# All casts of two weight matrices on GpSimd, no small copies on it in the first block, and a new order of the first block's steps

## The chip, the cores and the metric

The kernel runs on one core of a Trainium2 chip. Its engines are PE (TensorE: matrix products, with its weight loads as PEld), DVE (VectorE), ACT (ScalarE), POOL (GpSimd) and SP (SyncE, which here only issues loads). They run side by side, each takes its own instructions strictly in order, and they wait for each other by semaphores. The metric is the device time in microseconds, as the median of several runs, before and after the change. Matmul results land in PSUM; every other on-chip tensor lies in SBUF.

## What is computed

Retention (a decaying linear attention) over 4 batches, 8 heads, 768 positions in blocks of 64, and then a channel mix on its output `x`:

```python
x_prev = np.concatenate([np.zeros((B, 1, D)), x[:, :-1, :]], axis=1)
xk = mu_k * x + (1.0 - mu_k) * x_prev
xr = mu_r * x + (1.0 - mu_r) * x_prev
k = np.maximum(xk @ w_k, 0.0)              # 512 -> 1024
v = k * k @ w_v                            # 1024 -> 512
r = 1.0 / (1.0 + np.exp(-(xr @ w_r)))      # 512 -> 512
return r * v
```

## The kernel before

**Tiling.** The 768 positions go through in six blocks `n` of 128, each block for the four pairs of heads `hp`. The large products (`k_product`, `r_part`, `v_part`, lines 434, 423, 460) split each fp32 operand in a high and a low part and take three matmuls (high x high, high x low, low x high), so a matmul on `xl` needs the low part of the activation.

**The order.** Nothing is scheduled: the string `ORDER` (line 508) lists steps, a letter with two indices each, and the loop at line 494 issues them one after the other. All instructions of one engine stay in that order (the recording helper is line 33, so every row of the profile has that line). The letters used below, with the functions and what they put on which engine:

- `L`, `N`, `M`: loads of a pair's queries and keys, values, and keys by rows. SP issues all loads in one queue (`load_hp`, `load_qv`, `load_first`).
- `T0`, `T2` (`powers`, line 184): decay tables `Dt` and `LP`. PE transposes, DVE and ACT copy out.
- `A` scores on PE, `a` decay: in block 0 two DVE multiplications `mv<-sc,Dt` of a PSUM tile with `Dt`. `q` decays queries: DVE `mv<-qv,LP`, of two SBUF operands.
- `B` values on PE, `b` a copy of the result to SBUF (`raw<-xp`, ACT, block 0 alone), `k` ACT decays keys, `U` sums on PE, `u` state on ACT.
- `e`, `E` (`mix_prev`, line 392): ACT scales the attention output into `ts`, shifted by one column, for the k and the r branch; then POOL copies column 0 of `ts` from `lastw` (the last column of the block before) and saves the new last column in `lastw`. `f`, `F` (`mix`): DVE finishes `ts`. `y`, `x` (`split_x`): ACT writes the high part `xh`, DVE the low part `xl`; tiles 0 to 3 are the k branch's (`y`), 4 to 7 the r branch's (`x`).
- `S`, `c`, `C`, `D`: a weight is loaded as raw 16-bit words of its fp32 values (`S`), the upper halves are cast to fp16 into one of two tiles `top` (`conv_top`, line 245: `top<-raw`), DVE combines them by shift and OR (`conv_bits`: `raw<-raw,top`), and `split` makes high (ACT) and low part (DVE, `wk<-raw,wk` or `wr<-raw,wr`). Pieces k4 to k7 and r0 to r3 have 512 elements a partition, k2, k3 and v0 to v3 have 1024. Here POOL casts k4 to k7 and ACT casts the others.
- `G`, `K`: products with w_k, in block 0 pair by pair (`G`), `R`, `Q`: products with w_r, `V`: products with w_v.

There are two tiles `top`, taken in turn, so a cast waits for the OR of the cast two before it.

Of the kernel before, what the change touches and what calls it, by code (L numbers as in the profile page):

```python
# [7 lines left out]
F32 = mybir.dt.float32  # L8
# [7 lines left out]
ALU = mybir.AluOpType  # L16

B, H, S, D = 4, 8, 768, 64
HP = H // 2
NT = S // 128  # L20
# [16 lines left out]
def tile_retention_moe(  # L37
# [26 lines left out]
    tensor, vector, scalar, gpsimd, sync = (  # L64
        InOrder(tc, e) for e in (tc.nc.tensor, tc.nc.vector, tc.nc.scalar, tc.nc.gpsimd, tc.nc.sync))
# [6 lines left out]
    tiny = ctx.enter_context(tc.tile_pool(name="tiny", bufs=1))  # L72
# [22 lines left out]
    Dt = const.tile([128, H, 128], F32, name="Dt")  # L95
    LP = const.tile([128, HP, 64], F32, name="LP")
    LC = tiny.tile([128, HP], F32, name="LC")
    lastw = tiny.tile([128, 2, HP, B], F32, name="lastw")
    omu = tiny.tile([128, 2, HP], F32, name="omu")

    first = {}
# [72 lines left out]
    vector.tensor_tensor(rows.rearrange("p (c a) -> p c a", a=8), now[:, 8:25].rearrange("p (c o) -> p c o", o=1).broadcast_to([128, 17, 8]),  # L174
                         lows.rearrange("p (o a) -> p o a", o=1).broadcast_to([128, 17, 8]), op=ALU.mult)
    vector.tensor_scalar(omu, mus, -1.0, 1.0, op0=ALU.mult, op1=ALU.add)
    gpsimd.memset(lastw, 0.0)
    gpsimd.tensor_copy(lone[:, 512:640].rearrange("p (a x) -> p a x", a=2),
                       parity.rearrange("p (a o) -> p a o", o=1).broadcast_to([128, 2, 64]))

# [42 lines left out]
    def part(kind, i):  # L223
        if kind == "r" or i >= 4:
            j, c = divmod(i % 4, 2)
            c = slice(c, c + 1)
        else:
            j, c = i, slice(0, 2)
        key = f"{kind}{j}"
        if key not in raw:  # L230
            raw[key] = home(RAW[key], "raw", True)
        return key, c, raw[key].rearrange("p (c x) -> p c x", c=2)[:, c]
# [8 lines left out]
    def tops_of(kind, i, t):  # L241
        top = tops[turn.setdefault((kind, i), len(turn) % 2)]
        return top[:, 0:t.shape[1] * 512].rearrange("p (c o) h -> p c o h", o=512)

    def conv_top(kind, i):
        t = part(kind, i)[2]
        copy = gpsimd.tensor_copy if kind == "k" and i >= 4 else scalar.copy
        copy(tops_of(kind, i, t)[:, :, :, 1].bitcast(F16), t[:, :, 2::4].bitcast(BF16))

    def words(t):  # L250
# [13 lines left out]
    scs, mvs, us, xps, ts = {}, {}, {}, {}, {}  # L264
# [127 lines left out]
    def mix_prev(n, which, hp):  # L392
        ts[n, which, hp] = t = tiny.tile([128, B, 129], F32, tag=f"ts{which}", name="ts", bufs=2)
        scalar.activation(t[:, :, 1:129], xps[n, hp], AF.Copy, scale=omu[:, which, hp:hp + 1])
        gpsimd.tensor_copy(t[:, :, 0], lastw[:, which, hp, :])
        if n + 1 < NT:
            gpsimd.tensor_copy(lastw[:, which, hp, :], t[:, :, 128])

    def mix(n, which, hp):
        t = ts[n, which, hp]  # L400
        o = t[:, :, 0:128]
        vector.scalar_tensor_tensor(o, xps[n, hp], mus[:, which, hp:hp + 1], t[:, :, 0:128],
                                    op0=ALU.mult, op1=ALU.add)
# [17 lines left out]
    rps, rt, kps, kfs, k2, vps = {}, {}, {}, {}, {}, {}  # L421
# [60 lines left out]
    def v_out(n, b):  # L482
# [3 lines left out]
    steps = dict(  # L486
        L=load_hp, N=load_qv, A=scores, a=decay, q=decay_queries, k=decay_keys, U=sums, u=even_state, w=odd_state, B=values,
        e=lambda n, hp: mix_prev(n, 0, hp), E=lambda n, hp: mix_prev(n, 1, hp),
        f=lambda n, hp: mix(n, 0, hp), F=lambda n, hp: mix(n, 1, hp),
        y=lambda n, hp: split_x(n, 0, hp), x=lambda n, hp: split_x(n, 1, hp),  # L490
        M=lambda n, hp: load_first(hp, 2), b=keep_raw, G=lambda f, hp: k_product(0, f, hp),
        R=lambda n, hp: r_part(n, hp, 0), Q=lambda n, hp: r_part(n, hp, 1), s=r_out, K=k_part, h=k_square, p=k_split, V=v_part, o=v_out,
        S=stage_part, c=conv_top, C=conv_bits, D=conv_split)
    for step in ORDER.split():
        if step[0] == "T":
# [3 lines left out]
        else:  # L499
            i, j = step[1], int(step[2])  # L500
# [5 lines left out]
CUTS = ((0, 1024, 2048), (0, 1024, 1536, 2048), (0, 1024, 1536, 2048), (0, 1024, 1536, 2048))  # L506

ORDER = """
L00 Z10 L01 M00 M03 T0 k00 Sk4 A00 A01 L02 T2 a00 a01 k03 ck4 M01 B00 A02 Ck4 b00 e00 N01 E00 f00 N02 U00 a02 B01 L03 F00 Dk4
y00 u00 B02 k01 A03 b01 Sk5 x00 N03 M02 G20 G00 b02 ck5 Sk6 Sk7 E01 a03 G30 Ck5 e01 e02 f01 F01 E02 B03 Dk5 y01 f02 G10 ck6 b03  # L510
U01 Ck6 ck7 k02 Ck7 G11 e03 x01 y02 Sk2 G21 Dk6 G31 f03 U02 u01 Sk3 Dk7 U03 G01 ck2 Ck2 E03 G22 y03 Sr1 ck3 G32 Ck3 G02 G12 G33
Sr0 G23 Sr3 Sv3 Dk2 F02 cr1 Dk3 G13 G03 h03 cr0 Sr2 F03 h02 Cr1 Sv0 h00 cr3 Cr0 N11 Sv1 p01 Dr1 cr2 K07 K05 Dr0 h01 Cr3 Cr2 h05
x02 Dr2 Dr3 x03 K04 p00 h04 u03 Q00 N10 h07 Q01 cv0 Sv2 cv3 u02 q11 Q02 Cv0 Q03 L11 Cv3 Dv0 R00 s03 R01 cv1 Cv1 L10 Dv3 R02 k10
R03 K06 k11 s01 A10 A11 q10 Dv1 cv2 Cv2 U10 L12 p02 h06 U11 Dv2 L13 p03 s02 u11 N13 a10 V04 a11 V02 w11 V03 V05 N12 k13 B11 s00
u10 B10 o01 V00 E11 w10 o02 k12 e11 q13 U13 A12 N20 A13 U12 L20 V06 V01 E10 q12 e10 u12 a12 F11 x11 L21 V07 u13 k20 k21 f10 f11
a13 F10 B13 B12 w13 y10 y11 E13 e13 N21 N22 e12 w12 A20 o03 o00 f12 f13 y12 y13 U21 U20 q21 A21 F13 L22 K10 K11 a20 u20 K13 a21
h11 x13 h10 u21 q20 k22 K14 h13 K12 p10 K15 w20 L23 w21 k23 E12 N23 F12 U22 U23 x10 A23 h12 A22 B20 h15 p11 a23 h14 x12 B21 Q10
E21 L30 e20 L31 Q11 Q12 E20 f20 u22 F20 F21 k31 Q13 s12 s13 q23 K17 h17 K16 N31 e21 N30 R10 h16 R11 R12 p12 u23 w22 x21 k30 p13
# [80 lines left out]
```

## Time and profile before

| | |
|---|---|
| median of 3 runs | 397.16 us (396.19 to 399.07) |
| the profiled execution: time, span | 395.83 us, 394.0 us |
| PE busy | 387.8 us (98% of the span), granted clock 1.0 throughout |
| DVE, ACT, POOL busy | 244.3 us (62%), 201.5 us (51%), 34.4 us (9%) |
| the chain that ended last | PE 94%; products with w_v 34%, w_k 32%, w_r 17% |

The span is the time from the first to the last instruction of one execution; 1.8 us lie around it. The chain of waits that ended last is PE itself from 24 us on; only in the first 24 us do other engines and loads stand in it. A row of the timeline gives start and duration in us, engine, line, operation, output<-inputs, shapes, the number of instructions merged in it, and in brackets the engine's idle time before it and what ended that.

### The profile page before, as it was taken

The page shows a single profiled execution, that of the slowest core. Times are in us where ns is not written, and L with a number is a line of the kernel's source. Part 1 is how long each engine was busy: PE and PEld are TensorE (multiplying, and loading weights), DVE is VectorE, ACT ScalarE, POOL GpSimd, SP SyncE. Part 2 cuts the span into 40 slices and gives each one's busy share as a digit, 9 for nine tenths or more (in the row PEclk, how much of TensorE's full clock was granted, in tenths as well). Part 3 has the DMA queues.
Part 4 walks back from the last instruction along what each step waited for, and adds up shares of the span by engine and source line. Part 5 has one row for each costly group of instructions (what it writes and reads, how often), then busy time and mean ns, then how long its engine had stood idle before and what let it go on. Part 6 is the DMA issues. An engine that isn't in the chain of part 4 may idle for free.

```text
span 394.0 us, 8421 instructions
## 1 busy us (share of the span) xinstructions
PE 387.8 (98%) x3532; PEld 321.4 (82%) x3532; DVE 244.3 (62%) x392; ACT 201.5 (51%) x367; POOL 34.4 (9%) x104
## 2 busy tenths in 40 slices
PE   8899999999999999999999999999999999999996
PEld 5777888888888888888888888888888888888886
DVE  6987898699857375876565285855456844222411
ACT  4989997575755362475612347721266542222400
POOL 6540000100110010100100010210000000000000
PEclk9999999999999999999999999999999999999999
DMA  8998934654250081250701070340100001000002
GB/s 302 411 352 300 352 109 137 201 143 166 69 150 0 30 238 57 62 154 0 209 34 57 27 208 8 109 134 27 53 2 2 2 2 55 27 27 2 0 28 80
DMA packets 13606, 42.58 MB, mean 108 GB/s; under 512 B 1920, under 2 KB 2304, under 8 KB 13568
## 3 DMA queue, kind: packets, MB, share of 16 engines
q1 hardware_dynamic: 9824, 35.68, 28.2%
q10 hardware_dynamic: 3744, 6.36, 4.4%
q8 instruction: 28, 0.46, 0.5%
q14 instruction: 10, 0.08, 0.1%
HBM read 35.74 MB, written 6.29 MB: 107 GB/s over the span
## 4 chain that ended last, share of the span: by engine, by line
PE 94%; DVE 1%; POOL 1%; ACT 1%; issue 1%; DMA 0%; POOLq 0%; DVEq 0%
PE vp L33 34%; PE kp L33 32%; PE rp L33 17%; PE xp L33 5%; PE sc L33 3%; PE u L33 3%; POOL lastw L33 1%; PE table L33 0%; DMA smalls<-small 0%; POOL ts L33 0%; ACT ts L33 0%; DVE xl L33 0%; DVE raw L33 0%; POOL pows L33 0%; POOL top L33 0%
## 5 line engine op out<-in xcount | busy, mean ns | idle before, releaser
L33 PE MATMUL vp<-wv,k 128*128 128x512 f32 (+1 forms) x600 | 134.5, 382 | 0.0
L33 PEld LDWEIGHTS vp<-wv,k 128*128 128x128 f32 x600 | 108.9, 188 | 21.9 <-ACT kf L33 0.2
L33 PE MATMUL kp<-xh,wk 128*128 128x512 f32 x384 | 123.3, 391 | 0.0
L33 PEld LDWEIGHTS kp<-xh,wk 128*128 128x128 f32 x384 | 72.1, 188 | 15.7 <-ACT kf L33 0.4
L33 PE MATMUL kp<-xl,wk 128*128 128x512 f32 x192 | 75.0, 390 | 0.0
L33 PE MATMUL rp<-wr,xh 128*128 128x512 f32 x192 | 59.5, 391 | 0.0
L33 DVE TENSOR_TENSOR kf<-kf 128x512 f32<-128x512 f32 x40 | 27.3, 691 | 51.9 <-ACT kf L33 51.7
L33 ACT ACTIVATE kf<-kp 128x512 f32<-128x512 f32 x48 | 28.2, 594 | 54.3 <-PE kp L33 37.8
L33 ACT COPY qv<-st 64x256 f32<-64x256 f32 x80 | 32.4, 405 | 27.4 <-DVE st L33 23.4
L33 DVE TENSOR_TENSOR xl<-ts,xh 128x512 fp32r<-128x512 f32 x48 | 32.5, 688 | 22.0 <-ACT xh L33 21.9
L33 ACT CAST xh<-ts 128x512 fp32r<-128x512 f32 x48 | 29.2, 617 | 28.8 <-DVE rt L33 23.4
L33 PEld LDWEIGHTS kp<-xl,wk 128*128 128x128 f32 x192 | 36.0, 188 | 7.8 <-DVE xl L33 0.6
L33 PEld LDWEIGHTS rp<-wr,xh 128*128 128x128 f32 x192 | 35.8, 188 | 7.5
L33 DVE TENSOR_TENSOR rt<-vp,rt 128x512 f32<-128x512 f32 (+1 forms) x25 | 16.4, 665 | 38.4 <-PE vp L33 38.4
L33 PE MATMUL rp<-wr,xl 128*128 128x512 f32 x96 | 37.4, 390 | 0.0
L33 ACT ACTIVATE ts<-xp,omu 128x512 f32<-128x512 f32 x40 | 26.2, 688 | 18.5 <-PE xp L33 16.9
L33 DVE TENSOR_TENSOR mv<-qv,LP 64x256 f32<-64x256 f32 x80 | 33.6, 421 | 1.5
L33 DVE TENSOR_TENSOR k<-kf,k 128x1024 fp32r<-128x1024 f32 x24 | 29.3, 1225 | 8.1 <-ACT k L33 7.8
L33 DVE SCALAR_TENSOR_TENSOR ts<-xp,smalls,ts 128x512 f32<-128x512 f32 x40 | 29.2, 746 | 7.5 <-ACT ts L33 7.1
L33 DVE TENSOR_TENSOR mv<-sc,Dt 64x512 f32<-64x512 f32 (+1 forms) x48 | 32.5, 686 | 1.1 <-ACT Dt L33 0.5
L33 ACT ACTIVATE rt<-rp 128x512 f32<-128x512 f32 x24 | 14.0, 594 | 30.7 <-PE rp L33 30.7
L33 POOL COPY ts<-lastw 128x4 f32<-128x4 f32 x48 | 15.6, 327 | 138.2 <-DVE xl L33 138.2
(66 smaller groups left out, 294.2 us busy)
## 6 DMA issues: line engine op xcount, KB each, us to landing
qv<-qv SPq DMA_DIRECT2D x40, 256.0 KB, 6.1
kin<-kk SPq DMA_DIRECT2D x20, 512.0 KB, 5.7
out<-rt ACTq DMA_DIRECT2D x23, 256.0 KB, 2.0
raw<-w_v SPq DMA_DIRECT2D x4, 1023.8 KB, 7.2
in<-parts SPq DMA_DIRECT2D x5, 512.0 KB, 5.5
raw<-w_k SPq DMA_DIRECT2D x2, 1023.8 KB, 11.7
raw<-k_half SPq DMA_DIRECT2D x4, 511.8 KB, 8.1
raw<-w_r SPq DMA_DIRECT2D x4, 511.8 KB, 12.2
```

The costliest lines, as they stand in the source:

```text
L33: return lambda *args, **kw: self.tc.keep_in_program_order(op(*args, **kw))
```

## The change

The change has three parts. `conv_top` now puts the casts of k2, k3 and r0 to r3 on POOL as well, so that POOL makes all ten casts of w_k and w_r. `mix_prev` no longer chains two small POOL copies: ACT saves the unscaled last column in `lastx` (k branch's step alone, both halves of the buffer in turn), POOL multiplies it by `omu` into column 0 of `ts` from block 1 on, and in block 0 DVE writes zeros there. And `ORDER` is rewritten for block 0 and the start of block 1; the mixes and splits of pairs 2 and 3 for the r branch and the sums `U02` and `U03` stand later.

```diff
-    lastw = tiny.tile([128, 2, HP, B], F32, name="lastw")
+    lastx = tiny.tile([128, 2, HP, B], F32, name="lastx")
...
-    gpsimd.memset(lastw, 0.0)
...
-        copy = gpsimd.tensor_copy if kind == "k" and i >= 4 else scalar.copy
+        copy = gpsimd.tensor_copy if f"{kind}{i}" in "k4 k5 k6 k7 k2 k3 r0 r1 r2 r3".split() else scalar.copy
...
         scalar.activation(t[:, :, 1:129], xps[n, hp], AF.Copy, scale=omu[:, which, hp:hp + 1])
-        gpsimd.tensor_copy(t[:, :, 0], lastw[:, which, hp, :])
-        if n + 1 < NT:
-            gpsimd.tensor_copy(lastw[:, which, hp, :], t[:, :, 128])
+        if which == 0 and n + 1 < NT:
+            scalar.copy(lastx[:, n % 2, hp, :], xps[n, hp][:, :, 127])
+        if n == 0:
+            vector.memset(t[:, :, 0], 0.0)
+        else:
+            gpsimd.tensor_tensor(t[:, :, 0], lastx[:, (n - 1) % 2, hp, :], omu[:, which, hp:hp + 1].broadcast_to([128, B]), op=ALU.mult)
...
-L00 Z10 L01 M00 M03 T0 k00 Sk4 A00 A01 L02 T2 a00 a01 k03 ck4 M01 B00 A02 Ck4 b00 e00 N01 E00 f00 N02 U00 a02 B01 L03 F00 Dk4
...
+L00 Z10 L01 A00 Sk4 T0 A01 M00 L02 T2 a00 B00 ck4 k00 a01 b00 N02 A02 N01 E00 L03 U00 e00 Ck4 Sk5 u00 N03 a02 f00 B01 Sk6 Dk4
...
```

On POOL, before, from the copy of `LC` (made with the table `T2`) on:

```order
L33 COPY LC<-LP 128x4
L33 CAST top<-raw 128x512
L33 COPY ts<-lastw 128x4
L33 COPY lastw<-ts 128x4
L33 COPY ts<-lastw 128x4
L33 COPY lastw<-ts 128x4
L33 CAST top<-raw 128x512
```

On POOL, of the change, from the same copy on:

```order
L33 COPY LC<-LP 128x4
L33 CAST top<-raw 128x512 x4
L33 CAST top<-raw 128x1024 x2
L33 CAST top<-raw 128x512 x4
L33 TENSOR_TENSOR ts<-lastx,omu 128x4 x40
```

The ten casts now follow each other with nothing between them, and the six new ones stand ahead of every small operation of the later blocks.

On DVE, before, the end of the r branch's preparation in block 0 (`xl7` is the last low part that block 0's products with w_r need; `wr0`, `wr1` are halves of w_r, `k2_1` a squared k for w_v):

```order
L33 SCALAR_TENSOR_TENSOR raw_431<-raw_431,top_116 128x512 x2
L33 TENSOR_TENSOR k2_1_490<-kf_469,k2_1_490 128x2x512
L33 TENSOR_TENSOR wr0_493<-raw_431,wr0_493 128x512 x2
L33 SCALAR_TENSOR_TENSOR raw_451<-raw_451,top_116 128x512 x2
L33 TENSOR_TENSOR xl6_92<-ts_333,xh6_84 128x512
L33 TENSOR_TENSOR wr1_534<-raw_451,wr1_534 128x512 x2
L33 TENSOR_TENSOR xl7_93<-ts_422,xh7_85 128x512
L33 TENSOR_TENSOR k2_0_554<-kf_480,k2_0_554 128x2x512
L33 TENSOR_TENSOR mv_585<-qv1_485,LP_99 64x4x64 x4
```

On DVE, of the change, up to the same `xl7`:

```order
L33 SCALAR_TENSOR_TENSOR raw_379<-raw_379,top_116 128x512
L33 TENSOR_TENSOR xl6_92<-ts_459,xh6_84 128x512
L33 TENSOR_TENSOR wr0_505<-raw_379,wr0_505 128x512
L33 TENSOR_TENSOR k2_1_508<-kf_430,k2_1_508 128x2x512
L33 SCALAR_TENSOR_TENSOR raw_421<-raw_421,top_116 128x512
L33 TENSOR_TENSOR wr0_505<-raw_379,wr0_505 128x512
L33 SCALAR_TENSOR_TENSOR raw_421<-raw_421,top_116 128x512
L33 TENSOR_TENSOR mv_546<-qv0_427,LP_99 64x4x64 x4
L33 TENSOR_TENSOR wr1_559<-raw_421,wr1_559 128x512 x2
L33 TENSOR_TENSOR xl7_93<-ts_463,xh7_85 128x512
```

The four multiplications `mv<-qv,LP` of step `q10` moved ahead of `xl7`; `k2_0` stays behind it.

On PE, before, the start after the warm-up products:

```order
L33 MATMUL table<-eye,rows 128x128 x8
L33 MATMUL sc<-in 128x128 x16
L33 MATMUL table<-lone 128x256
L33 MATMUL xp<-mv,in 64x128 x8
L33 MATMUL sc<-in 128x128 x8
```

On PE, of the change, the same place:

```order
L33 MATMUL sc<-in 128x128 x8
L33 MATMUL table<-eye,rows 128x128 x8
L33 MATMUL sc<-in 128x128 x8
L33 MATMUL table<-lone 128x256
L33 MATMUL xp<-mv,in 64x128 x8
```

The scores `A00` of pair 0 moved ahead of the eight transposes of the decay table.

## Rows read from the trace of the kernel before

**Rows 1.** Windows of the span: busy us by engine, clock, DMA share, GB/s.

```profile
core 0: us, PE busy (x) PEld busy (x) DVE busy (x) ACT busy (x) POOL busy (x), PEclk, DMA share, GB/s
120.00:200.00 80.00, 80.00 (x874) 67.09 (x873) 51.58 (x85) 41.15 (x79) 4.92 (x24) 1.00 0.32 93
7.27:43.43 36.16, 34.19 (x279) 27.19 (x276) 31.29 (x45) 34.39 (x60) 11.46 (x22) 1.00 0.96 356
24.70:390.90 366.20, 366.20 (x3302) 305.49 (x3299) 224.53 (x353) 182.95 (x330) 18.54 (x74) 1.00 0.29 91
```

**Rows 2.** Timeline of PE, 4 to 45 us: start, duration, instructions, idle before.

```profile
4.78 1.29 PE L33 MATMUL table<-eye,rows 128*128 128x128 f32 x8
6.00 2.06 PE L33 MATMUL sc<-in 64*128 64x128 f32 x32
...
10.98 1.16 PE L33 MATMUL sc<-in 64*128 64x128 f32 x16 [1.27 <-DMA in<-parts]
...
24.08 0.69 PE L33 MATMUL u<-in 128*64 128x64 f32 x16 [0.71 <-ACT st L33]
...
39.59 0.61 PE L33 MATMUL rp<-wr,xh 128*128 128x512 f32 x2
...
44.13 0.39 PE L33 MATMUL rp<-wr,xl 128*128 128x512 f32 x1
```

**Rows 3.** Timeline of DVE, 0 to 50 us, same columns.

```profile
0.88 0.07 DVE L33 MEMSET steps<- 128x8 f32 x1
...
5.67 0.76 DVE L33 COPY Dt<-table 128x128 f32<-128x128 f32 x2 [0.87 <-PE table L33]
6.35 0.42 DVE L33 TENSOR_TENSOR lone<-rows,smalls 128x256 f32<-128x256 f32 x1
...
17.05 0.69 DVE L33 SCALAR_TENSOR_TENSOR raw<-raw,top 128x512 uint32<-128x512 uint32 x1
...
19.57 0.69 DVE L33 TENSOR_TENSOR xl<-ts,xh 128x512 fp32r<-128x512 f32 x1
...
36.43 1.23 DVE L33 TENSOR_TENSOR k<-kf,k 128x1024 fp32r<-128x1024 f32 x1 [1.99 <-ACT k L33]
...
40.93 0.69 DVE L33 TENSOR_TENSOR xl<-ts,xh 128x512 fp32r<-128x512 f32 x1 [0.87 <-ACT xh L33]
...
42.75 0.68 DVE L33 TENSOR_TENSOR xl<-ts,xh 128x512 fp32r<-128x512 f32 x1
...
44.71 1.72 DVE L33 TENSOR_TENSOR mv<-qv,LP 64x256 f32<-64x256 f32 x4
```

**Rows 4.** Timeline of DVE, 21.9 to 22.9 us: one OR alone.

```profile
21.97 1.13 DVE L33 SCALAR_TENSOR_TENSOR raw<-raw,top 128x512 uint32<-128x512 uint32 x1 [1.04 <-POOL top L33]
```

**Rows 5.** Timeline of POOL, 9 to 23 us.

```profile
9.67 0.76 POOL L33 CAST top<-raw 128x512 f16<-128x512 bf16 x1 [0.33 <-DMA raw<-k_half]
...
15.48 1.10 POOL L33 CAST top<-raw 128x512 f16<-128x512 bf16 x1 [3.19 <-DMA raw<-k_half]
...
18.51 1.80 POOL L33 COPY lastw<-ts 128x4 f32<-128x4 f32 x1
...
21.16 1.45 POOL L33 CAST top<-raw 128x512 f16<-128x512 bf16 x2
```

**Rows 6.** Timeline of ACT, 0 to 32 us.

```profile
2.47 0.20 ACT L33 ACTIVATE one<-one 128x1 f32<-128x1 f32 x1
...
12.80 0.37 ACT L33 COPY st<-u 128x256 f32<-128x256 f32 x1
...
24.44 1.38 ACT L33 CAST top<-raw 128x1024 f16<-128x1024 bf16 x1
...
29.00 0.78 ACT L33 CAST top<-raw 128x512 f16<-128x512 bf16 x1
```

**Rows 7.** Timeline of SP, and landing of the first loads (`in`).

```profile
1.17 1.84 SPq L33 DMA_DIRECT2D in<-parts  x4
...
DMA to landing us min/median/max: 3.9/7.4/9.0
```

More of the change, by code (lines that the diff above doesn't have):

```diff
@@ L508 @@
 ORDER = """
-L00 Z10 L01 M00 M03 T0 k00 Sk4 A00 A01 L02 T2 a00 a01 k03 ck4 M01 B00 A02 Ck4 b00 e00 N01 E00 f00 N02 U00 a02 B01 L03 F00 Dk4
[L510 to L515, printed above, removed]
+L00 Z10 L01 A00 Sk4 T0 A01 M00 L02 T2 a00 B00 ck4 k00 a01 b00 N02 A02 N01 E00 L03 U00 e00 Ck4 Sk5 u00 N03 a02 f00 B01 Sk6 Dk4
+A03 y00 B02 M01 b01 ck5 G10 G20 e01 Sk7 b02 M02 a03 Sk2 f01 Sk3 Ck5 e02 F00 ck6 B03 y01 Dk5 b03 G30 G00 k01 f02 Ck6 e03 ck7 U01
+Ck7 G01 G31 y02 G11 G21 Dk6 M03 Sr0 Sr1 G32 E01 k02 f03 F01 Dk7 G22 y03 ck2 u01 G02 Ck2 x00 G33 G12 x01 ck3 G13 k03 Sr3 Ck3 Dk2
+N10 h03 G23 U02 cr0 Sr2 U03 Dk3 E02 F02 E03 G03 K04 Sv0 cr1 Cr0 F03 Cr1 h02 K05 x02 Dr0 p01 u03 cr3 Sv1 Cr3 cr2 Sv3 h01 K07 Dr1
+N11 h00 h05 Cr2 q10 R00 Dr2 Dr3 R01 L11 cv0 x03 Cv0 h04 R02 R03 K06 cv3 u02 Cv3 s01 s00 Dv0 cv1 Cv1 k11 Sv2 q11 Dv3 Q00 Q01 Q02
+L10 Q03 p00 cv2 Cv2 k10 U11 U10 Dv1 h07 A10 p02 Dv2 A11 a11 s03 V04 h06 p03 s02 L13 V02 k13 u10 V03 u11 V05 N12 a10 L12 w11 w10
+B11 E11 B10 N13 o01 V00 o02 k12 e11 q13 U13 A12 N20 A13 U12 L20 V06 V01 E10 q12 e10 u12 a12 F11 x11 L21 V07 u13 k20 k21 f10 f11
 a13 F10 B13 B12 w13 y10 y11 E13 e13 N21 N22 e12 w12 A20 o03 o00 f12 f13 y12 y13 U21 U20 q21 A21 F13 L22 K10 K11 a20 u20 K13 a21
```

## The prediction

> **What bounds the kernel now.** I read the windows first: from 24.7 to 390.9 us PE is busy for all 366.20 us of 366.20, at a granted clock of 1.00 [rows 1]. What PE does there doesn't change (same products, same operands), so the change can move the time only through what makes PE wait in block 0. The timeline of PE shows those waits: it starts real work at 4.78 us, behind the warm-up products; it idles 1.27 us for a load and 0.71 us at 24.08 us for ACT [rows 2]. That is 1.98 us that could be saved behind the start, 0.5% of the profiled execution's 395.83 us. Gains are bounded by that; losses are not.
>
> Next, who is close behind PE? In the stretch from DVE's first `mv<-sc,Dt` (7.27 us) to the end of `xl7` (42.75 + 0.68 = 43.43 us) DVE is busy 31.29 and ACT 34.39 of 36.16 us [rows 1, 3]. So ACT is nearly full and DVE has 36.16 - 31.29 = 4.87 us of idle time, the longest pieces being 1.99 us for ACT's `k` and 0.87 us for ACT's `xh` [rows 3]. And PE is only a little behind them: the products with w_r begin at 39.59 us, and the first one that needs `xl7` runs at 44.13 us [rows 2], 0.70 us after `xl7` is there. This is the place to watch: whatever delays the end of `xl7` by more than 0.70 us delays PE by the rest, and PE has no idle time afterwards in which to catch up.
>
> The last view is POOL's timeline beside DVE's. A cast of 512 elements takes 0.76 us when DVE is idle, and two in a row 1.45 [rows 5]. But the OR at 21.97 us, which begins while the second of those casts runs (21.16 + 1.45 - 0.76 = 21.85 us), takes 1.13 us where the OR at 17.05 takes 0.69 [rows 3, 4]: it stood still for 0.44 us. The other way round, POOL's copy of four elements at 18.51 took 1.80 us and ended at 20.31, just as DVE's `xl` (19.57 + 0.69 = 20.26) ended [rows 3, 5]. And the cast at 15.48 took 1.10 us [rows 5]. So on this chip DVE's operations of two SBUF operands and POOL's reads of SBUF don't run together here; one waits for the other.
>
> The Trainium skill says so too ("SBUF — State Buffer", section "Who interferes with whom"): a DVE instruction with two SBUF inputs contends with a GpSimd instruction that reads SBUF, and the lock is held for the full instruction. By that last clause the OR at 21.97 should have begun to run only at the cast's end, 22.61, and ended at 23.30; the row has 23.10, so the trace agrees on the lock and not quite on its length.
>
> **The change, part by part.**
>
> *Casts off ACT.* ACT loses two casts of 1024 elements and four of 512: 2 x 1.38 + 4 x 0.78 = 5.9 us [rows 6]. It gains a `lastx` copy of four elements for each pair, four in block 0 and sixteen later. No row shows one; I bound it by the 0.20 us of a one-element ACTIVATE and the 0.37 us of a 256-element copy [rows 6], so 0.8 to 1.5 us in block 0. ACT, the fullest of the three, is relieved by about 4.7 us net, and stops being what DVE waits for.
>
> *Casts on POOL.* Nothing but casts stands there in block 0. Each reads SBUF, and holds DVE's two-operand operations: from the cast's start at 21.85 until the OR ran (22.41 = 21.97 + 1.13 - 0.69) that is 0.56 us for 512 elements [rows 4, 5], and I take twice, 1.12 us, for 1024 (no row; below it one 512-cast's 0.56, above it 1.45, the time of two whole casts). How many of the ten meet DVE at such work? Placing them by their loads and by the OR that frees their `top`: k4 and k5 fall beside `mv<-sc,Dt`, which has only one SBUF operand, and cost nothing (0 is the lower bound of the others as well). k6, k7, k2, k3 and r0 to r3 fall where DVE's order is a closed row of ORs, `wk`, `wr`, `xl` and `ts`, all with two SBUF operands. That is 6 x 0.56 + 2 x 1.12 = 5.6 us that DVE stands still, against 0.44 before. If POOL loses each race instead of winning it, the casts come later and the ORs wait for them, which costs about the same.
>
> *Removed small copies.* They cost DVE nothing visible; POOL's waits on them end. In block 0 eight DVE memsets take their place: 8 x 0.07 = 0.56 us [rows 3]. In later blocks POOL's multiplication has bounds of 0.19 us (the shortest copies) and 1.80 us [rows 5], and ACT's sixteen `lastx` copies come to 16 x 0.37 = 5.9 us at most. Both lie under PE: in the window 120 to 200 us POOL is busy 4.92, ACT 41.15 and DVE 51.58 us of 80 [rows 1]. If that cover were gone, a late `ts` would cost PE its whole lateness; nothing in the window suggests it.
>
> *New order, the start.* `A00` now stands ahead of `T0`. The first load is issued at 1.17 us and lands 3.9 us later, at 5.07 [rows 7]; so PE starts 5.07 - 4.78 = 0.29 us later, and `T0` comes 0.29 + 1.03 (half of the 2.06 us of 32 score records [rows 2]) = 1.32 us later. DVE's copies of `Dt` follow: 5.67 + 1.32 = 6.99, and its first `mv` 6.35 + 0.42 - 5.67 less the 0.06 us of overlap, 1.04 us, behind: 8.03 us instead of 7.27 [rows 3]. On SP's queue the loads of `M03` (256 KB) no longer stand ahead of `L02`; at 356 GB/s [rows 1] that brings the scores of pair 2 forward by 0.26 / 0.356 = 0.7 us, out of the 1.27 us of PE's wait. Other loads move (keys of pairs 1 to 3 behind the k weights, `N10` ahead of r and v weights), but none so far that PE or a cast would wait longer than DVE makes it.
>
> *New order, later.* Steps of equal work change places, but one thing moves ahead of `xl7` on DVE: the four `mv<-qv,LP` of `q10`, 1.72 us [rows 3]. On PE the same amount of work as before stands ahead of the first product with `xl7` (all of `G`, `K04`, `K05`, `K07`, and three of four pairs of one half of w_r's products).
>
> **The sum.** DVE's end of `xl7`, new: start 8.03, plus the work of the old stretch without its standstill, 31.29 - 0.44 = 30.85, plus memsets 0.56, plus `q10` 1.72, plus standstills 5.6, plus its own idle time. Of that 4.87 us I keep 0.5: the pieces were waits for ACT and for POOL's casts, and DVE, now later than both, won't have them (bounds 0 and 4.87; near the lower end, as ACT is 4.7 us less loaded). 8.03 + 30.85 + 0.56 + 1.72 + 5.6 + 0.5 = 47.26 us. PE ran this product at 44.13; now it runs at about 47.29. That is +3.2 us, and the 0.7 us won at the start is swallowed in it. Behind it the next thing that could hold PE, the preparation of w_v on DVE, has the same work in both; I set it at 0.
>
> 395.83 + 3.2 = 399.0 us for the profiled execution. It stands 1.33 us below the median 397.16; on the median the sum is 400.4, and allowing that the median of three may lie a little high I say **400.0 us**, 0.7% slower. About 1% (4 us) is what a measurement here can tell from no change, so this forecast is "same".
>
> **Rivals.**
>
> *A, the casts hide.* If they mostly fall beside one-operand work or in pauses, DVE's standstill is near 0 to 2.5 us and `xl7` is ready by 41.7 to 44.2 us, in time. Then the start decides: +0.29 - 0.7 and up to -0.71 for the wait at 24.08, whose sums now stand further back: -1.1 to 0, 396.0 to 397.2 us. For it: of the four casts before, only one held DVE up. Against: of DVE's 4.87 us of idle time 1.99 and 0.87 us lie behind 34 us [rows 3], too late for the casts of k6, k7, k2 and k3.
>
> *B, the standstill is longer.* If a 512-cast holds DVE for its whole 0.76 us and a 1024-cast for 1.45 [rows 5], the eight cost 6 x 0.76 + 2 x 1.45 = 7.5 us, 1.9 more: +5.1, 402.3 us, slower by 1.3%. It decides where the standstills pass 6.4 us (4.0 us of delay). For it: POOL's casts must also wait for DVE (1.10 instead of 0.76), and each such wait delays an OR, then ACT's `wk`. Against: the one row that shows DVE waiting has 0.56. The Trainium skill's clause on the full instruction, in the section named above, speaks for this rival; by it the time is this 402.3.
>
> *C, ACT's relief counts.* If DVE were not the next bound, ACT's 4.7 us could come to PE; but PE has only 1.98 us to get back, so 395.2 us at best. Faster by over 1% (393.2) is out of reach.
>
> **Chances.** The forecast (+1.5 to +4) 0.48, A 0.24, B with its neighbours 0.26, C 0.02. Range: A's lower end leaves little out below 396.0; above, B reaches 402.5 with some 0.1 beyond. The forecast's own range is 398.7 to 401.1. Faster by over 1%: 0.02; within 1%: 0.71; slower: 0.27, B and the upper edge of the forecast.
>
> **What would show it.** Right: ORs, `wk` and `xl` on DVE of 1.1 to 1.3 us (1.8 for those beside 1024-casts) between 17 and 40 us; DVE almost without idle time from 8 to 47 us; `xl7` ending near 47.3; PE idle for DVE, some 4 to 5 us in total between 19 and 47 us, where before it waited 1.27 and 0.71; nothing new behind 60 us. Wrong: DVE's rows at 0.69 throughout (A), casts of k2 and k3 far over 1.5 us and `xl7` past 48 us (B), or PE waiting for POOL or a load.

## The result, and the profile after

The changed kernel takes **398.81 us** (median of 14 runs, 398.46 to 400.10) against 396.12 us of the kernel before, measured beside it (median of 14). The ratio is 1.0063, with a 95% interval of 1.0049 to 1.0077: 2.5 us slower by the ratio, and within 1% of before. 400.0 us was forecast, on a median of before of 397.16; 0.7% was the forecast loss and 0.63% the measured one. The profiled execution of the changed kernel took 398.82 us with a span of 397.0; before, it was 395.83 with 394.0.

The windows of after, in the columns of [rows 1] (busy us of PE, PEld, DVE, ACT, POOL, then the granted clock, the DMA share and GB/s):

```profile
20.00:30.00 10.00, 7.95 (x45) 5.88 (x45) 10.00 (x14) 7.36 (x16) 4.26 (x4) 1.00 1.03 368
7.27:43.43 36.16, 33.33 (x269) 25.29 (x270) 35.01 (x53) 29.45 (x57) 14.39 (x13) 1.00 0.90 338
24.70:390.90 366.20, 364.00 (x3302) 302.47 (x3303) 227.69 (x356) 182.61 (x346) 21.40 (x45) 1.00 0.29 91
```

In the stretch 7.27 to 43.43 us DVE went from 31.29 to 35.01 us busy and ACT from 34.39 to 29.45 [rows 1]: DVE and ACT have changed places. From 20 to 30 us DVE is busy all the time and PE only 7.95 us of 10 (8.96 and 9.29 in before). Where PE was busy 366.20 us of 366.20, it now is 364.00. The granted clock is 1.00 in all three windows. From 120 to 200 us PE is busy 80.00 us of 80 in both kernels.

The timeline of PE in after, to be held against [rows 2] (start, duration, instructions, idle before):

```profile
4.57 1.62 PE L33 MATMUL sc<-in 64*128 64x128 f32 x16
6.12 1.09 PE L33 MATMUL table<-eye,rows 128*128 128x128 f32 x8
...
9.52 1.09 PE L33 MATMUL xp<-mv,in 128*64 128x128 f32 x16 [0.59 <-DMA in<-parts]
...
23.93 0.39 PE L33 MATMUL kp<-xl,wk 128*128 128x512 f32 x1
24.82 0.73 PE L33 MATMUL kp<-xh,wk 128*128 128x512 f32 x2 [0.50 <-DVE ts L33]
...
26.32 0.61 PE L33 MATMUL kp<-xh,wk 128*128 128x512 f32 x2
28.42 0.50 PE L33 MATMUL kp<-xl,wk 128*128 128x512 f32 x1 [1.49 <-DVE xl L33]
...
44.64 0.39 PE L33 MATMUL rp<-wr,xh 128*128 128x512 f32 x1
45.62 0.50 PE L33 MATMUL rp<-wr,xh 128*128 128x512 f32 x1 [0.59 <-DVE wr L33]
...
47.34 0.39 PE L33 MATMUL rp<-wr,xl 128*128 128x512 f32 x1
```

The load wait of 1.27 us at 10.98 and ACT's 0.71 us at 24.08 are gone; a load wait of 0.59 us is left, and three waits for DVE are new, 2.58 us by their brackets. The brackets leave something out: products follow each other every 0.227 us where nothing holds them (in before, 24 products from 39.59 to 45.03), and a row ends about 0.16 us after the next could start. By the distances of the starts the three stalls are 24.82 - 23.93 - 0.23 = 0.66, 28.42 - 26.32 - 2 x 0.227 = 1.65 and 45.62 - 44.64 - 0.23 = 0.75 us, 3.06 in all, and ten small ones of 0.07 to 0.22 us between 24 and 46 us add 1.2 (in before such small ones add 0.5). The product at 47.34 is the first that needs `xl7`. Before, it stood at 44.13 [rows 2], so it comes **3.21 us** later, and the last product ends 3.1 us later (394.01 against 390.91). All of the loss is there by 47 us.

The chain of work that ended last says which of the waits decides. Followed back from the end, it is PE alone down to 45.62 us, and DVE alone for a long way before that (start, duration, what):

```profile
44.42 0.42 DVE mv L33
...
44.87 0.70 DVE wr L33
...
45.62 2.79 PE rp L33 x11
```

So the last thing that holds PE is DVE's `wr` behind `q10`, the first of the two operations right ahead of `xl7`. The two stalls at 24.82 and 28.42 us are real, but had they been shorter with DVE as late as it is, PE would only have waited longer at 45.62. `xl7` itself ends at 46.77, 0.57 us before its product.

The timeline of DVE in after, to be held against [rows 3, 4]:

```profile
7.82 2.48 DVE L33 TENSOR_TENSOR mv<-sc,Dt 128x512 f32<-128x512 f32 x4
...
11.94 1.29 DVE L33 TENSOR_TENSOR mv<-sc,Dt 128x512 f32<-128x512 f32 x2 [0.90 <-PE sc L33]
...
15.19 0.68 DVE L33 TENSOR_TENSOR mv<-sc,Dt 128x512 f32<-128x512 f32 x1
15.21 0.06 DVE L33 MEMSET ts<- 128x4 f32 x1
...
17.05 1.20 DVE L33 SCALAR_TENSOR_TENSOR raw<-raw,top 128x512 uint32<-128x512 uint32 x1
...
20.04 1.19 DVE L33 SCALAR_TENSOR_TENSOR ts<-raw,smalls,ts 128x512 f32<-128x512 f32 x1
...
22.98 1.79 DVE L33 TENSOR_TENSOR wk<-raw,wk 128x512 fp32r<-128x512 f32 x1
...
25.36 1.79 DVE L33 SCALAR_TENSOR_TENSOR ts<-raw,smalls,ts 128x512 f32<-128x512 f32 x1
...
29.42 1.80 DVE L33 TENSOR_TENSOR xl<-ts,xh 128x512 fp32r<-128x512 f32 x2
...
32.28 2.87 DVE L33 TENSOR_TENSOR wk<-raw,wk 128x1024 fp32r<-128x1024 f32 x2
...
37.22 1.21 DVE L33 SCALAR_TENSOR_TENSOR raw<-raw,top 128x512 uint32<-128x512 uint32 x1
...
38.96 1.19 DVE L33 TENSOR_TENSOR wr<-raw,wr 128x512 fp32r<-128x512 f32 x1
...
43.12 1.72 DVE L33 TENSOR_TENSOR mv<-qv,LP 64x256 f32<-64x256 f32 x4
...
46.08 0.69 DVE L33 TENSOR_TENSOR xl<-ts,xh 128x512 fp32r<-128x512 f32 x1
```

Eight rows are longer than their operation alone (0.69 for an OR, 0.74 for a `ts`, 0.68 for `wk`, `xl` and `wr` of 512; 1.28 and 2.42 for the two pairs, as the run with six memsets below has them). The rest is standstill: 0.51 at 17.05 (cast of k6), 0.45 at 20.04 (k7), 1.11 at 22.98 (k2), 1.05 at 25.36 (k3), and 0.52, 0.45, 0.52 and 0.51 for the four casts of r. Together **5.12 us**. The casts beside them, on POOL's timeline of after ([rows 5] for before):

```profile
9.53 0.78 POOL L33 CAST top<-raw 128x512 f16<-128x512 bf16 x1
14.73 1.16 POOL L33 CAST top<-raw 128x512 f16<-128x512 bf16 x1 [4.42 <-DMA raw<-k_half]
16.69 1.07 POOL L33 CAST top<-raw 128x512 f16<-128x512 bf16 x1 [0.80 <-DMA raw<-k_half]
...
22.70 1.59 POOL L33 CAST top<-raw 128x1024 f16<-128x1024 bf16 x1 [1.95 <-DMA raw<-w_k]
25.19 1.49 POOL L33 CAST top<-raw 128x1024 f16<-128x1024 bf16 x1 [0.91 <-DMA raw<-w_k]
```

Read them against each other. The cast of k5 (14.73 to 15.89) lies beside `mv<-sc,Dt` at 15.19, which has one operand in SBUF and takes its usual 0.68. The other way round, the cast of k6 begins at 16.69 while a `ts` runs (16.39 to 17.13); that `ts` takes its usual 0.74, and the cast takes 1.07 where 0.76 is its time alone. The cast of k2 ends at 24.29; the `wk` that began at 22.98 ends at 24.77, so its own 0.68 us began at 24.09, 0.20 before the cast's end. For k6 the same count gives 17.56 against 17.76, again 0.20, and for k3 26.41 against 26.68, 0.27. So DVE is held from its arrival until shortly before the cast's end. How shortly is less sure, since the profile's spans on POOL are rough.

### The profile page after: what moved, and what is told of

The parts are those of the page before. It is cut to its first block, busy times and chain, and to the rows that moved or that the text cites. A ratio compares the mean times of both kernels' runs of the same rounds, so it can differ in the third digit from the quotient of the medians.

```text
span 397.0 us, 8360 instructions
## 1 busy us (share of the span) xinstructions
PE 389.6 (98%) x3532; PEld 321.5 (81%) x3532; DVE 248.9 (63%) x400; ACT 199.0 (50%) x381; POOL 32.8 (8%) x61
## 2 busy tenths in 40 slices
DMA packets 13606, 42.58 MB, mean 107 GB/s; under 512 B 1920, under 2 KB 2304, under 8 KB 13568
## 4 chain that ended last, share of the span: by engine, by line
PE 88%; DVE 6%; DMA 2%; issue 2%; ACT 1%; SPq 1%; DVEq 0%
PE vp L33 33%; PE kp L33 28%; PE rp L33 16%; PE xp L33 5%; PE sc L33 3%; PE u L33 3%; DMA in<-parts 2%; DVE raw L33 1%; DVE wk L33 1%; DVE ts L33 1%; DVE xl L33 1%; DVE wr L33 1%; DVE mv L33 1%; SPq L33 1%; ACT raw L33 0%
## 5 line engine op out<-in xcount | busy, mean ns | idle before, releaser
L33 POOL TENSOR_TENSOR ts<-lastx,omu 128x4 f32<-128x4 f32 x40 | 14.7, 378 | 275.2 <-DVE xl L33 275.2
```

The lines of the kernel that those rows point to most:

```text
L33: return lambda *args, **kw: self.tc.keep_in_program_order(op(*args, **kw))
```

## The experiments

The theory was the prediction's: the casts on POOL hold DVE's two-operand operations, DVE becomes the last to be ready for block 0's products, and PE loses what DVE loses beyond its slack. The rivals: the new order costs the time whatever the casts do; the new column of the previous token (`lastx`, memsets on DVE) costs it; the later start costs it. Each ratio below is against the kernel before on the same chip in the same set of runs; its medians were 396.73, 396.22, 396.42 and 396.45 us in the four sets.

**Casts that read nothing.** A memset takes POOL about as long as a cast takes alone, but reads nothing. The upper halves of six pieces are left out of the computation by it.

```diff
-        copy(tops_of(kind, i, t)[:, :, :, 1].bitcast(F16), t[:, :, 2::4].bitcast(BF16))
+        top = tops_of(kind, i, t)[:, :, :, 1].bitcast(F16)
+        if f"{kind}{i}" in "k2 k3 r0 r1 r2 r3".split():
+            gpsimd.memset(top, 0.0)
+        else:
+            copy(top, t[:, :, 2::4].bitcast(BF16))
```

> The changed kernel with the six new casts on POOL (k2, k3, r0 to r3) replaced by a POOL memset of the same part of the same tile; the casts' values are left out, order and waits stay. A memset writes SBUF and reads nothing. Theory (POOL's reads of SBUF stop DVE's operations of two SBUF operands): the DVE rows beside these six fall from 1.2 and 1.8 us to 0.69, xl7 ends some 4 us earlier (about 43 us), and the time is about 4.0 us below the changed kernel, 394.8 to 395.5 us, a little under the kernel before. Rival (the new order, with its later start and q10 ahead of xl7, is what costs): at most 1 us below the changed kernel. Rival (POOL's casts are late themselves and the ORs wait for them): the gain is only what the memset is shorter by on POOL, under 1.5 us.

Measured: 395.35 us, ratio 0.9969 [0.9953, 0.9984]. That is 3.7 us less than after by the ratios ((1.0063 - 0.9969) x 396), and 1.2 us less than before. Its DVE timeline, first beside the cast of k6, which it keeps, then at the places of memsets:

```profile
17.02 1.20 DVE L33 SCALAR_TENSOR_TENSOR raw<-raw,top 128x512 uint32<-128x512 uint32 x1
...
23.02 0.68 DVE L33 TENSOR_TENSOR wk<-raw,wk 128x512 fp32r<-128x512 f32 x1
...
27.30 1.28 DVE L33 TENSOR_TENSOR xl<-ts,xh 128x512 fp32r<-128x512 f32 x2
...
29.64 2.42 DVE L33 TENSOR_TENSOR wk<-raw,wk 128x1024 fp32r<-128x1024 f32 x2
```

And POOL beside it:

```profile
21.95 2.47 POOL L33 MEMSET top<- 128x1024 f16 x2 [1.81 <-DVE ts L33]
27.43 0.70 POOL L33 MEMSET top<- 128x512 f16 x1 [3.02 <-DVE raw L33]
```

The `wk` at 23.02 runs inside POOL's two memsets and takes its 0.68 us, while the OR beside the cast that was kept still takes 1.20. `xl7` ends at 42.92 instead of 46.77. Two limits: the memsets are shorter than the casts were beside DVE (0.70 us against 1.17 to 1.70 for 512 elements, 2.47 for two of 1024 against 1.59 and 1.49), and a memset doesn't wait for the load whose data the cast would read, so that of k2 begins at 21.95 and not at 22.70, though the OR behind it still waits for the load. The rival that POOL's casts are merely late allowed 1.5 us for this; 3.7 came back.

**The other four casts too.** The same edit with all ten pieces in the list, so that the casts of k4 to k7 are memsets as well.

> After with all ten GpSimd casts of the weights replaced by a memset of the same region that reads nothing (the casts' values are left out of the computation). With six of them replaced it ran 395.35 us; the other four are k4 to k7, of which k6 and k7 stood VectorE for 0.5 us each in every kernel so far, k4 and k5 hardly. Standstill theory: 1 us less, 394.0 to 394.8. The rival that k4 to k7 fall into room that VectorE has there anyway expects 395.1 to 395.6.

Measured: 394.82 us, ratio 0.9965 [0.9951, 0.9978]. By the ratios that is 0.2 us less than with six, by the medians 0.5; the median lies just above the theory's range. The traces say where the rest went. The first product with `xl7` runs at 42.58 here and at 43.60 with six memsets, so in block 0 the casts of k6 and k7 do cost 1.0 us. But the last product ends only 0.28 us earlier (390.28 against 390.56). The chain of this run shows what stands behind block 0:

```profile
32.15 11.04 DMA raw<-w_v
...
43.27 1.36 ACT top L33
...
52.77 0.62 PE u L33 x26
```

A load of w_v lands at 43.20, ACT's cast of it begins at 43.27, and over ACT's next casts that reaches PE at 52.77. With six memsets this load lands at 42.53, and ACT doesn't wait for it. So the six new casts are what costs the time of after, and this load lets only 0.3 of the further 1.0 us through.

**The casts back on ACT.** The new order and the new column stay.

```diff
-        copy = gpsimd.tensor_copy if f"{kind}{i}" in "k4 k5 k6 k7 k2 k3 r0 r1 r2 r3".split() else scalar.copy
+        copy = gpsimd.tensor_copy if f"{kind}{i}" in "k4 k5 k6 k7".split() else scalar.copy
```

> The changed kernel, new order and lastx, with the six new casts back on ACT. Theory: the standstills of DVE beside them go (about 4.2 us), but ACT gets 5.9 us of casts back in an order that was written without them, and now ACT is late for the products; it ends within 1 us of the changed kernel, 398 to 400 us. Rival (standstills alone decide): 394.5 to 395.5 us. Rival (the order alone costs, whoever casts): 398.8 us too, but then e1 would be slow as well, which tells the two apart.

Measured: 399.30 us, ratio 1.0072 [1.0056, 1.0088], no better than after. PE's timeline shows a different cause:

```profile
34.89 0.73 PE L33 MATMUL kp<-xh,wk 128*128 128x512 f32 x2 [0.53 <-DVE ts L33]
...
40.62 0.50 PE L33 MATMUL kp<-xh,wk 128*128 128x512 f32 x1 [1.65 <-ACT kf L33]
```

ACT is busy 37.20 us from 8 to 48 us (33.36 in after), and PE waits 1.65 us for ACT's `kf`. So in the new order the work of the six casts is too much for ACT, and on POOL it is too much for DVE, at a price that these runs can't tell apart.

**The casts on POOL in the old order.** Before, with the list of after for the casts and nothing else.

> The kernel before, its order and its small copies, with only the six casts moved to POOL. Theory: the standstills come with the casts, so it is slower than the kernel before by about 2 us (398 us), less than the changed kernel since DVE has its pauses (4.9 us) in the old order. Rival (only the new order costs): the same as before or faster, as ACT is relieved of 5.9 us.

Measured: 399.92 us, ratio 1.0087 [1.0071, 1.0103]: +3.4 us by the ratio where 2 were expected. PE's timeline:

```profile
11.70 1.16 PE L33 MATMUL sc<-in 64*128 64x128 f32 x16 [1.54 <-DMA in<-parts]
...
31.51 0.50 PE L33 MATMUL kp<-xl,wk 128*128 128x512 f32 x1 [1.32 <-DVE xl L33]
34.74 0.50 PE L33 MATMUL kp<-xh,wk 128*128 128x512 f32 x1 [0.40 <-ACT kf L33]
```

It is the wait of after again, a `kp<-xl` for DVE's `xl`, behind the casts of k2 and k3. The loss doesn't need the new order. The miss in size has two parts. The scores of pair 2, which wait for a load, came 0.72 us later than before (11.70 against 10.98 [rows 2]), which no cast explains; in two other runs below with this order of loads they came at 10.79 and 11.46. And DVE's pauses did not take up the standstills: the rows beside the casts of k2, k3, r0 and r1 are 1.11, 1.11, 0.52 and 0.45 us too long, 3.19 in all, before DVE's first pause behind them. PE waited for ACT's `kf` as well, which stands on ACT behind a cast `wk` that had waited 1.21 us for DVE's OR.

**Only k2 and k3 back on ACT.**

```diff
-        copy = gpsimd.tensor_copy if f"{kind}{i}" in "k4 k5 k6 k7 k2 k3 r0 r1 r2 r3".split() else scalar.copy
+        copy = gpsimd.tensor_copy if f"{kind}{i}" in "k4 k5 k6 k7 r0 r1 r2 r3".split() else scalar.copy
```

> After with the casts of k2 and k3 alone put back on ScalarE; r0 to r3 stay on GpSimd. The standstill theory: the two 1024-element casts held VectorE 1.05 to 1.10 us each in after's rows, the four 512-element casts of r 0.45 to 0.52 each, and the earliest product that waited (1.49 us for an xl, at 28.42 us) stands right behind the two long ones. Taking these two away frees 2.1 us of VectorE; ScalarE pays about 1.5 us for them in a stretch where it has room (7.4 of 10 us busy from 20 to 30 us). So about 1.3 us below after: 397.2 to 398.0. The rival that the new order is the cause whatever the casts do expects 398.6 to 399.3, as it was when all six went back to ScalarE.

Measured: 397.71 us, ratio 1.0033 [1.0021, 1.0044], inside the standstill theory's range. The two long standstills and the 1.49 us wait behind them are gone, and 1.2 us by the ratios with them. ACT has room for two of the six casts, not for six.

**The new column alone, and everything but it.** Two runs: after with `lastw` and its small POOL copies as before (its cut is below), and before with `lastx`, the memsets and the products of after.

```diff
...
-        if which == 0 and n + 1 < NT:
-            scalar.copy(lastx[:, n % 2, hp, :], xps[n, hp][:, :, 127])
-        if n == 0:
-            vector.memset(t[:, :, 0], 0.0)
-        else:
-            gpsimd.tensor_tensor(t[:, :, 0], lastx[:, (n - 1) % 2, hp, :], omu[:, which, hp:hp + 1].broadcast_to([128, B]), op=ALU.mult)
+        gpsimd.tensor_copy(t[:, :, 0], lastw[:, which, hp, :])
+        if n + 1 < NT:
+            gpsimd.tensor_copy(lastw[:, which, hp, :], t[:, :, 128])
```

> After with the column of the previous token handled as before (lastw on GpSimd, two small copies for each piece, no memset on VectorE). The prediction charged the eight memsets on VectorE 0.56 us and the small GpSimd copies nothing. The standstill theory: VectorE gets 0.56 us back, but the two small copies of each piece come back to GpSimd between the casts, where one of them can again take over a microsecond; the net is within 0.5 us of after, 398.3 to 399.3. The rival that the new column is what cost the time expects before's time, 396 to 397.

Measured: 398.90 us, ratio 1.0067 [1.0054, 1.0080], as after.

> Before with the new column of the previous token alone (lastx, memset on VectorE in block 0, the product on GpSimd later); casts and order as before. VectorE gets eight memsets of 0.07 us, ScalarE sixteen small copies of about 0.2 us over the stages, GpSimd loses its copies. Expected 0 to 0.6 us above before: 396.4 to 397.0. The rival that the small copies held VectorE (a hold taken away when they go) expects 0.5 to 1.5 us below before.

Measured: 396.54 us, ratio 1.0012 [0.9995, 1.0028]. The new column costs nothing that can be told from zero in either surrounding.

**The start.** After with `T0` again ahead of `A00`, where before had it.

```diff
-L00 Z10 L01 A00 Sk4 T0 A01 M00 L02 T2 a00 B00 ck4 k00 a01 b00 N02 A02 N01 E00 L03 U00 e00 Ck4 Sk5 u00 N03 a02 f00 B01 Sk6 Dk4
+L00 Z10 L01 T0 A00 Sk4 A01 M00 L02 T2 a00 B00 ck4 k00 a01 b00 N02 A02 N01 E00 L03 U00 e00 Ck4 Sk5 u00 N03 a02 f00 B01 Sk6 Dk4
```

> After with step T0 (the copy of the tables that VectorE's first products need) ahead of A00, where before had it; nothing else moves. The prediction charged 0.76 us of its 3.2 to VectorE starting later behind A00. If the start is a term of the sum, it falls by about 0.7 us: 398.0 to 398.4. If the start is swallowed on the way (VectorE stood 0.90 us for the scores on TensorE at 11.94 us in after, and it waits at L02's data either way), it stays within 0.3 us of after: 398.5 to 399.1.

Measured: 398.82 us, ratio 1.0064 [1.0051, 1.0076], the same as after. DVE's first `mv` starts at 7.24 instead of 7.82, then waits 0.67 us for scores at 11.43; `xl7` ends 0.51 us earlier, its first product runs 0.51 us earlier (46.83), and the profiled span is 0.3 us shorter. The intervals of the two ratios are as wide as that, so the medians can't say whether it is a gain.

**`q10` behind `xl7`.** After with the step `q10` moved from between `Cr2` and `R00` to right behind `x03`.

> The changed kernel with step q10 (four DVE multiplications, 1.72 us) behind x03, where xl7 is made. My sum charged q10 with its full 1.72 us ahead of xl7. If the terms add up as I wrote, xl7 ends 1.7 us earlier and the time falls by 1.2 to 1.7 us, to about 397.3. If something else is ready no earlier (ACT's xh for xl7, ACT's high part of w_r), it falls by less than 0.5 us, and q10 only filled a gap.

Measured: 398.85 us, ratio 1.0070 [1.0052, 1.0088], no change. The timelines of DVE and PE:

```profile
43.39 1.29 DVE L33 TENSOR_TENSOR wr<-raw,wr 128x512 fp32r<-128x512 f32 x2 [0.69 <-ACT wr L33]
45.66 0.69 DVE L33 TENSOR_TENSOR xl<-ts,xh 128x512 fp32r<-128x512 f32 x1 [0.98 <-ACT xh L33]
46.39 1.72 DVE L33 TENSOR_TENSOR mv<-qv,LP 64x256 f32<-64x256 f32 x4
...
46.41 0.50 PE L33 MATMUL rp<-wr,xl 128*128 128x512 f32 x1
```

Without `q10` ahead of it DVE waits 0.69 and 0.98 us for ACT, 1.67 of the 1.72 us saved. ACT's `wr` had waited for DVE's OR, and its `xh` stands behind that `wr` and a cast of w_v of 1.37 us. PE did gain: its wait for `wr` is gone, and the first product with `xl7` runs at 46.41, 0.93 us earlier than in after. Some 0.4 us of that are an earlier front of this execution (28.03 against 28.42 us at the wait for `xl`). But at the products with w_v, 61.36 us here, only 0.25 are left, lost in small waits of PE from 56 us on. What ends those waits the profile doesn't name; `q10` now stands ahead of DVE's ORs for w_v.

**A version that might beat before.** Three runs put single pieces of the change into before: r2 and r3 on POOL, `M03`'s load behind `L02` (with `k03`, which needs it, ahead of `k02`), and both.

> Before with the casts of r2 and r3 alone moved from ScalarE to GpSimd; order and small copies as before. All six moved in this order cost 3.2 us; the standstill theory puts that on the two 1024-element casts of k2 and k3 (1.05 to 1.10 us each, right ahead of a product that waited 1.32 us) and on k7, r0 and r1 in the stretch where VectorE has no idle time. r2 and r3 come where VectorE has waited for ScalarE in before, so their 0.5 us each falls into that wait and ScalarE's relief of 1.5 us comes through: 395.0 to 396.0, 0.3 to 1.0 us below before. If a cast on GpSimd costs VectorE's 0.5 us wherever it stands, it is 396.8 to 397.3, 0.5 to 1.0 above before.

Measured: 396.16 us, ratio 0.9997 [0.9989, 1.0006]. Neither range was met: the median is 0.16 us above the lower one, and there is no gain. The profile says what the expectation overlooked. `xl7` ends at 42.66 instead of 43.43, but PE had no idle time behind 24.7 us in before to give back, and has none here.

> Before with the load step M03 (256 KB) moved from ahead of the third piece's load L02 to right behind it, and the step k03 that needs it to right ahead of k02; casts and all else as before. TensorE stood 1.27 us for L02's data at 10.98 us in before and 0.71 us at 24.08 us, and never again up to the end. If the earlier landing pays, about 0.7 us of the 1.27 goes, and the time falls to 395.4 to 395.9. If the gain is swallowed before 24 us, because VectorE's and ScalarE's work and the casts' data arrive no earlier, TensorE only waits elsewhere: 396.0 to 396.6.

Measured: 396.03 us, ratio 0.9981 [0.9964, 0.9999]. The median lies in the range for a gain that is swallowed.

> The two edits together that could each help before: M03 and k03 later, as in the run with these alone, and the casts of r2 and r3 on GpSimd (that alone measured 0.26 us below before, within the noise). TensorE is full behind 24.7 us in before, so the second edit can only take away lateness that the first one uncovers. Expected 0.3 to 0.8 us below before if the front's gain comes through, 395.5 to 396.0; the same as before, within 0.2 us, if it does not.

Measured: 396.11 us, ratio 0.9987 [0.9970, 1.0005], between the two ranges. The earlier load is there in the profile of the first of the two: the scores of pair 2 run at 10.15 us without a wait, and the 1.27 us wait at 10.98 is replaced by 0.18 us at 13.41 for ACT and by

```profile
12.14 1.09 PE L33 MATMUL xp<-mv,in 128*64 128x128 f32 x16 [0.21 <-DMA in<-parts]
...
24.14 0.69 PE L33 MATMUL u<-in 128*64 128x64 f32 x16 [0.72 <-ACT st L33]
```

but the wait for ACT's `st`, 0.71 at 24.08 before, is still 0.72 at 24.14. ACT arrives there no earlier, and what PE gained at the load it has lost by 13.4 us: from there on its products run within 0.05 us of before's. Whether the 0.2% of the medians is a gain can't be told from these runs; adding the casts to it adds nothing. No version here that does the whole work beats before by more than that.

## Why the prediction was right, and where its terms were off

**The bound right, the wait two operations off.** PE has no idle time behind 60 us in either kernel, the loss is complete when the first product with `xl7` runs, and DVE has taken ACT's place (38.69 us busy of 40 from 8 to 48 us in after, against 34.20 before). The product was put at 47.29 us and ran at 47.34; +3.2 us was forecast for the profiled execution, and it took 2.99 more. PE's stalls between 19 and 47 us were put at 4 to 5 us; by the starts they are 4.3. But the sum let PE wait for `xl7`, and the wait that decides is the one for `wr` at 45.62, which the sum did not have. That `wr` stands two operations ahead of `xl7` in DVE's closed sequence, so the mechanism holds. That the product came within 0.05 us of its forecast is luck: `xl7` was 0.49 us early, and its product ran 0.57 us behind it, where 0.03 was put. The work on w_v behind it, put at 0, held nothing in after. The runs with ten memsets and with `q10` later show that it holds PE as soon as block 0 is ready about 1 us earlier.

**The standstills: right, a little small.** 6 x 0.56 + 2 x 1.12 = 5.6 us were forecast, 5.12 are on the rows: 0.45 to 0.52 for a cast of 512, mean 0.49, and 1.05 and 1.11 for one of 1024. The doubling for 1024, for which before had no row, held. The placement held too, k4 and k5 at nothing and the eight others at DVE's two-operand work. That they cause the loss was argued in the prediction and is shown by the memsets: POOL at work in the same order without its reads gives 3.7 us back, and the two long casts taken off POOL give back 1.2.

**The sum of DVE's time: right by errors that cancel.** Forecast: start 8.03, 38.73 of work and standstill, 0.5 idle, end 47.26. Measured: start 7.82, 37.73 busy, 1.22 idle, end 46.77. The scores of pair 0 began at 4.57, 0.50 us before the 5.07 that was put, but PE was on them for 1.55 us and not 1.03, so the transposes began at 6.12, as put (6.10). The start came earlier since DVE's copy followed them by 0.69 us, where 0.89 was taken from before. The 1.04 us from there to the first `mv` left out, without saying so, the 0.51 us that DVE waits there for ACT in before; in after it waits no more (7.82 - 6.81 = 1.01). Of the 1.00 us of busy time that was too much, 0.48 is the standstills. The rest is about the memsets' 0.56: all but the first two lie inside the row of the operation ahead of them, as at 15.21 inside 15.19, and take almost nothing. Idle time was underrated by 0.72, most of it the 0.90 us for scores at 11.94.

**One term doesn't add.** The prediction counted the later start (8.03 - 7.27 = 0.76 us) and `q10` (1.72 us) in full. Of the start, 0.58 us taken back at the first `mv` gave 0.51 at `xl7` in the profile, so it does pass through, though the medians don't show it. Of `q10`, 1.67 of the 1.72 us taken back became waits of DVE for ACT. In this stretch DVE and ACT wait for each other by turns, and a sum over DVE's work alone counts as work what would otherwise be a wait. The 0.5 us of idle time that the sum kept was thus tied to `q10`: without it, the idle time grows to nearly what it took away.

**Rival A (the casts hide): its price was nearly right, its condition false.** It put the time without standstills at 1.1 to 0 us below before. The run with six memsets is 1.2 us below, with PE's front waits at 0.61 and 0.57 us instead of 1.27 and 0.71.

**Rival B (whole-cast standstill): not paid.** It asked for 0.76 and 1.45 us; the rows have 0.49 and 1.08. The Trainium skill ("SBUF — State Buffer", section "SBUF: two separate sides") says that whichever of the two starts first gets the shared ports for its whole instruction. The rows bear that out in part: DVE began to run 0.20, 0.20 and 0.27 us before the end of the casts of k6, k2 and k3. But a DVE instruction is not stopped when a cast begins (the `ts` at 16.39); it is stopped if it comes while one runs, and the time from its arrival to shortly before the cast's end is less than the cast. The full duration as the price was wrong here, although the full duration as the length of the lock is nearly right.

**Rival C (ACT's relief): right that it could not bring much.** No version with casts moved off ACT, and with all ten still made, is faster than before beyond its interval. What the prediction did not say is that the new order needs the relief: with the six casts left on ACT it is as slow as after (+2.9 us by the ratio, against +2.5). And the old order with the casts on POOL loses 3.4. So each half of the change alone costs about what both cost together, and the 2.5 us can't be shared out between them. What the runs show is the mechanism inside after: there it is the casts' reads that hold DVE.

**Median against profiled execution.** The sum gave 400.4 on the median shown, 400.0 was said. The median of before, with more runs, is 396.12, 1.04 us lower, which is most of the distance from 400.0 to 398.81. The prediction also held that about 1% is what can be told from no change here. The intervals of these runs are 0.1 to 0.2% to either side, so the loss of 0.63% is clear of noise.

## What to carry to other kernels

Work moved to POOL is not free for DVE: count each cast that reads SBUF at the time from the arrival of DVE's next two-operand instruction to shortly before the cast's end (here 0.49 us on average for a cast that takes 0.76 alone), and ask what DVE's slack to PE is. To test such a standstill, replace the cast by a memset of the same region: most of the occupancy stays, the reads go, and the difference is the price, up to what the next limit lets through. Where two engines feed each other by turns, a term that is late by one of them replaces a wait for the other, so before adding it to a sum look at which wait it would fill; and where PE has no idle time left behind a point, nothing that becomes ready earlier behind that point can be a gain.

## What the runs showed of the hardware that was not expected

A memset on POOL doesn't hold DVE: a `wk` of 0.68 us ran inside two memsets of 2.47 us, where beside a cast of the same 1024 elements it took 1.79. Nor did a cast hold an operation of DVE with one operand in PSUM (`mv<-sc,Dt`, 0.68 us beside the cast of k5).

In the run with the old column, two waits of PE were followed by a lower granted clock. The windows of its profile:

```profile
26.00:28.00 2.00, 0.33 (x2) 0.08 (x1) 2.00 (x4) 1.79 (x4) 0.17 (x1) 0.93 1.09 340
28.00:30.00 2.00, 2.00 (x5) 1.62 (x6) 2.00 (x3) 1.09 (x3) 0.93 (x1) 0.50 0.99 211
30.00:32.00 2.00, 2.00 (x7) 1.38 (x6) 2.00 (x3) 1.32 (x4) 0.77 (x2) 0.72 0.83 209
```

PE had waited 0.56 and then 1.67 us, and from 28 to 30 us the granted clock was 0.50, the 1.2 GHz level; a pair of products took 1.05 us there instead of 0.62. In after, with waits of 0.50 and 1.49 us at the same place, the clock stayed at 1.00. The run's time was that of after (398.90 us), since PE had to wait for DVE behind it anyway: this execution has no wait for `wr`. One profiled execution shows it, with a mean clock of 0.995 over its span. Of the other four executions of this version three have 0.996; of after's fourteen, one has.
